# Inverse roots by one GpSimd power, front loads on two hardware DMA queues, and a written-out order per engine, in a fused attention and GELU-MLP kernel

## The chip, the core and the metric

The kernel runs on one core of a Trainium2 chip. The metric is device time in microseconds (us) from launch to end; the median of three runs is compared. The engines of the core are named as the profile names them: PE (TensorE matmuls; PEld its weight loads), DVE (VectorE), ACT (ScalarE), POOL (GpSimd) and SP (SyncE, which here only issues DMAs). Each engine works through its own list of instructions in order and waits for others by semaphores.

## The reference

What is computed, cut to its core (batch 8, 12 heads, sequence 448, head size 64; then 3584 tokens of 768, inner size 2048):

```python
def rmsnorm(x, g):
    rms = np.sqrt(np.mean(x * x, axis=-1, keepdims=True) + 1e-06)
    return x / rms * g
q_n, k_n = rmsnorm(q, g_q), rmsnorm(k, g_k)
scores = np.matmul(q_n, k_n.transpose(0, 1, 3, 2)) / np.sqrt(64)
attn = softmax(scores)
x = np.matmul(attn, v)            # heads side by side: (3584, 768)
h = x @ w_in                      # (768, 2048)
g = h * (1.0 / (1.0 + np.exp(-1.702 * h)))
out = g @ w_out                   # (2048, 768)
```

## The kernel before

Two heads of one batch form a pair; there are 48 pairs, six to a batch. The kernel is written as a list of small tasks. Each task names its engine, the tasks it depends on, a duration that a planner assumes, and the code that issues its instructions. `_Order.run` plays these tasks through with the assumed durations, always takes the ready task of lowest key on each engine, and issues instructions in that order. So the finished program is a static list on each engine; keys (`KEYS`), earliest times (`AT`) and a set of moved tasks (`ON`) steer it. Where the planner finds PE idle, `fill` (L1047) puts dummy matmuls of zeros.

Names of tasks for pair i (used in the texts below):

- L(i,0), L(i,1), L(i,2): load q, k, v from memory, 224 KB each (L1065, L1062), on SP's DMA queue; L(0,1) alone and the two tiny loads of g_q and g_k go out on ACT's queue.
- S: squares (ACT L1073, or POOL L1070 in two halves). R: sum over a row of 64 (DVE L1082). Q: inverse root. For pairs 0 to 5, one at a time, it is Ln and Exp on ACT (L1093, L1094); for later pairs, three at a time, a seed by integer arithmetic on DVE (L1101, L1103) and two Newton steps of four instructions on POOL (L1114 to L1117).
- N(i,0), N(i,1): q and k times the inverse root, to bfloat16 (L1124, on POOL or DVE). V: v to bfloat16 (L1134 DVE, L1137 POOL).
- T(i,0), T(i,1): transposes, on PE (L1147) for pairs 0 to 11, by DMA (L1159) later. KQ, K: copies of the transposed q and k out of PSUM, k times the gains (L1151, L1154).
- C: scores (PE L1194), E: their exponential (ACT L1204 for pairs 0 to 5, which are done in two halves h = 0, 1 of the queries; L1202 later), P: times v (PE L1215), O: division by the row sum (DVE L1225, L1226), B and X: transpose back and copy into the tokens' matrix xt (PE L1241 and DVE L1245, later by DMA L1248).
- WI(c), WO(c): four loads each of w_in and w_out with conversion to bfloat16, issued by POOL (L1396, L1402).
- F(b,m): first product for batch b, block m (PE L1429), H: tanh (ACT L1439), G: gate (DVE L1451). Then the second product (PE L1459, L1524), written in large part as Strassen-like products of sums, which DVE forms; copies out on ACT and DVE, stores on SP and ACT (L1482).

F(b,m) needs all six pairs of batch b. So at the start PE has only the attention of the first six pairs; from F(0,0) on, attention of later pairs stands between the products of earlier batches.

ACT's function table is loaded at the start (set 6, for Ln and Exp), again after the Q of pairs 0 to 5 (set 0, for Exp and tanh), and near the end (set 12, for the last GELU).

The functions around the change:

Of the kernel before, what the change touches and what calls it, by code (L numbers as in the profile page):

```python
# [19 lines left out]
class _Task:  # L20
    __slots__ = ("eng", "dur", "lat", "emit", "key", "after", "at", "takes", "left", "users", "end", "start", "lock", "widen", "moves", "rest", "there", "alt", "either")


OVERLAP = {"ACT": 95.0, "DVE": 90.0, "POOL": 45.0}


class _Order:

# [12 lines left out]
    def add(self, name, eng, dur, emit, key, deps=(), lat=100.0, at=0.0, takes=None,  # L41
            lock=False, widen=None, moves=None, alt=None, either=None):


        t = _Task()
        t.alt = alt

        lat += OVERLAP.get(eng, 0.0)
        if name in ON:
            eng, dur, lock = alt  # L50
        dur -= OVERLAP.get(eng, 0.0)
        if alt:
            t.alt = alt[0], alt[1] - OVERLAP[alt[0]], alt[2]
        t.eng, t.dur, t.lat, t.emit = eng, dur, lat, emit
        t.after, t.at, t.takes = tuple(deps), AT.get(name, at), takes
        t.users, t.end, t.lock, t.widen = [], None, lock, widen
        t.moves = moves
        t.either = either and (either[0], either[1] - OVERLAP[either[0]],
                               lat - OVERLAP.get(eng, 0.0) + OVERLAP[either[0]], either[2])
        t.key = KEYS.get(name, round(key, 3))  # L60
        self.tasks.append(t)
        self.named[name] = t

    def run(self):
        for t in self.tasks:
            t.left = 0
            for d in t.after:
                if d in self.named:
                    self.named[d].users.append(t)
                    t.left += 1  # L70
        ready = {}
        seq = 0
        events = []
        free = {}

        def push(t, when):
            nonlocal seq
            seq += 1
            heapq.heappush(events, (when, seq, t))

        for t in self.tasks:
            ready.setdefault(t.eng, [])
            free.setdefault(t.eng, 0.0)
            if t.left == 0:
                push(t, t.at)
        free.setdefault("POOL", 0.0)
        self.free, self.hold = free, 0.0
        now, emitted = 0.0, 0
        over = []

        queues = {"sw": [], "hw": [], "act": []}
        moved_to = 0.0

# [3 lines left out]
        def share(t):  # L97
            n = len(heads())
            if n != 2:
                return 1.0 / n  # L100
            return 0.65 if not queues["sw"] else 0.69 if t.eng == "POOL" else 0.47

        def next_moved():
            h = heads()
            when = [q[0].there for q in queues.values() if q and q[0].there > moved_to]
            when += [moved_to + t.rest / share(t) for t in h]
            return min(when) if when else None

        def move_to(now):
            nonlocal moved_to, seq  # L110
            while moved_to < now:
                n = next_moved()
                until = now if n is None else min(now, n)
                h = heads()
                for t in h:
                    t.rest -= (until - moved_to) * share(t)
                moved_to = until
                for q in queues.values():
                    while q and q[0].rest < 1e-3 and q[0].there <= moved_to:
                        t = q.pop(0)  # L120
                        t.end = moved_to + 500.0
                        seq += 1
                        heapq.heappush(over, (t.end, seq, t, False))

        while emitted < len(self.tasks):
            for eng, q in ready.items():
                while q and free[eng] <= now:
                    held = []
                    best = None
                    while q:  # L130
                        c = heapq.heappop(q)
                        if c[2].end is not None:
                            continue
                        if self._fits(c[2], now):
                            best = c[2]
                            break
                        held.append(c)
                    for c in held:
                        heapq.heappush(q, c)
                    if best is None:  # L140
                        break
                    if best.either and eng != best.eng:
                        best.eng, best.dur, best.lat, best.emit = best.either
                    best.either = None
                    if best.takes and best.takes[0] in self.loose:
                        held = self.slots[best.takes[0]][1]
                        self.got = min(self._open(best.takes[0], now),
                                       key=lambda j: held[j] and self.named[held[j]].end or 0.0)
                        held[self.got] = best.takes[1][0]
                    elif best.takes:  # L150
                        self.slots[best.takes[0]][1].extend(best.takes[1])
                    for name, n in best.widen or ():
                        self.slots[name][0] = n
                    if eng == "PE" and self.fill:
                        self.fill(now - free[eng], now)
                    best.emit()
                    emitted += 1
                    free[eng] = now + best.dur
                    if best.lock:
                        self.hold = free[eng]  # L160
                    best.start = now
                    seq += 1
                    heapq.heappush(over, (free[eng], seq, best, True))
                    if best.moves:
                        best.rest, best.there, best.end = best.moves, free[eng] + 1850.0, 1e12
                        queues[{"POOL": "sw", "ACTQ": "act"}.get(eng, "hw")].append(best)
                    else:
                        best.end = free[eng] + best.lat
                        seq += 1
                        heapq.heappush(over, (best.end, seq, best, False))  # L170
            nxt = []
            if events:
                nxt.append(events[0][0])
            if over:
                nxt.append(over[0][0])
            nxt += [f for f in list(free.values()) + [self.hold] if f > now]
            n = next_moved()
            if n is not None:
                nxt.append(n)
            assert nxt, "no task can start"  # L180
            now = max(now, min(nxt))
            move_to(now)
            while over and over[0][0] <= now:
                _, _, t, same = heapq.heappop(over)
                for u in t.users:
                    if (u.eng == t.eng and not u.either) == same:
                        u.left -= 1
                        if u.left == 0:
                            push(u, max(now, u.at))
            while events and events[0][0] <= now:  # L190
                _, _, t = heapq.heappop(events)
                seq += 1
                for eng in (t.eng, t.either[0]) if t.either else (t.eng,):
                    heapq.heappush(ready[eng], (t.key, seq, t))
        move_to(now + 1e6)
        return now

    def _open(self, name, now):
# [3 lines left out]
        back = [h and self.named[h].end for h in held]  # L202
        return [j for j, h in enumerate(held)
                if h is None or (back[j] is not None and back[j] <= now)]

    def _fits(self, t, now):

        if (t.lock and self.free["POOL"] > now) or (t.eng == "POOL" and self.hold > now):
            return False
        if not t.takes:  # L210
            return True
        if t.takes[0] in self.loose:
            return bool(self._open(t.takes[0], now))
        n, held = self.slots[t.takes[0]]
        for j in range(len(t.takes[1])):
            if len(held) + j >= n:
                back = self.named[held[j - n]]
                if back.end is None or back.end > now:
                    return False
        return True  # L220

KEYS = {
    'Lg': 22.65, 'g': -13.05, 'gT': -31.93, 'gG': -13.06, ('L', 0, 0): -4.25, ('L', 0, 1):
# [633 lines left out]
def kernel(  # L859
# [166 lines left out]
    def fill(idle, now):  # L1026
        if waiting:
            idle -= waiting.pop()
# [975 lines left out]
```

## Time and profile before

| | us |
|---|---|
| timed runs: median (lowest to highest of 3) | 418.61 (417.22 to 418.70) |
| profiled execution: span from first to last instruction | 417.8 |
| PE busy in it | 406.2 |
| DVE, ACT, POOL busy | 316.9, 297.8, 177.4 |
| 113 dummy matmuls of L1047, busy | 18.3 |

The profiled execution is one run apart from the timed ones; the profile gives its span, and no separate time around it. "Busy" of PE includes the dummy matmuls and the pipelined ends of matmuls. Data moved: 45.61 MB read from memory and 11.01 MB written.

### The profile page before, as it was taken

The numbers are of one execution on the slowest core, as the hardware profiler recorded it, in microseconds if no ns is written. First come the engines' busy times: TensorE is split into PE (matmuls) and PEld (weight loads), VectorE is DVE, ScalarE is ACT, GpSimd is POOL, SyncE is SP. The second block draws the span as 40 slices with busy tenths as digits, with TensorE's granted clock in tenths as the row PEclk, the third lists the DMA queues.
The fourth block names the chain that finished last, engine by engine and source line by source line (L and its number), as shares of the span: only waits on it lengthen the run. The fifth ranks groups of instructions, "written<-read, shape, count | busy, mean of one in ns | idle before, by whom it ended". The sixth has DMA issues, their size and how long they took to land.

```text
span 417.8 us, 10076 instructions
## 1 busy us (share of the span) xinstructions
PE 406.2 (97%) x3874; PEld 240.4 (58%) x3874; DVE 316.9 (76%) x640; ACT 297.8 (71%) x441; POOL 177.4 (42%) x271
## 2 busy tenths in 40 slices
PE   8799999999999999999999999999999999999996
PEld 6557876655555555565555555455555665555564
DVE  3968888859979879887898877788757699557432
ACT  4879778789978588966997658886887725773211
POOL 5784978491565047937447164664220000000000
PEclk9999999999999999999999999999999999999999
DMA  8999999966385789588874787855541231000323
GB/s 202 232 245 245 257 242 249 245 183 158 79 192 126 174 210 225 108 230 183 191 190 121 164 207 201 160 110 139 136 111 35 54 99 57 2 1 16 99 77 113
DMA packets 101716, 63.38 MB, mean 152 GB/s; under 512 B 54948, under 2 KB 101668, under 8 KB 101668
## 3 DMA queue, kind: packets, MB, share of 16 engines
q1 hardware_dynamic: 93520, 55.58, 56.0%
q0 software_dynamic: 7296, 6.29, 9.2%
q10 hardware_dynamic: 852, 0.87, 0.7%
q8 instruction: 30, 0.49, 0.5%
q14 instruction: 18, 0.15, 0.1%
HBM read 45.61 MB, written 11.01 MB: 136 GB/s over the span
## 4 chain that ended last, share of the span: by engine, by line
PE 75%; DVE 8%; DMA 4%; ACT 4%; POOL 4%; issue 4%; SPq 0%; DVEq 0%; POOLq 0%; ACTq 0%
PE w L1429 20%; PE w L1524 19%; PE o L1215 10%; PE sc L1194 9%; PE b L1524 5%; PE b L1813 4%; PE w L1813 4%; PE w L1459 3%; DMA rows<-in_k_dram 3%; DMA rows<-in_v_dram 2%; DVE ssq L1082 2%; ACT att L1204 1%; ACT att L1202 1%; POOL row L1124 1%; POOL sq L1070 1%
## 5 line engine op out<-in xcount | busy, mean ns | idle before, releaser
L1202 ACT ACTIVATE att<-sc 112x896 bf16<-112x896 f32 x168 | 145.4, 916 | 28.1 <-PE sc L1194 27.2
L1429 PE MATMUL w<-xt,w_in_s 128*128 128x448 bf16 (+1 forms) x672 | 119.8, 326 | 1.0 <-DVE xt L1245 0.9
L1429 PEld LDWEIGHTS <-w_in_s 128*128 128x128 bf16 x672 | 61.2, 98 | 43.0 <-issue 8.3
L1215 PEld LDWEIGHTS <-att 112*128 112x128 bf16 x1536 | 61.6, 98 | 28.0 <-issue 9.7
L1451 DVE SCALAR_TENSOR_TENSOR g<-th,w 128x448 bf16<-128x448 f32 x96 | 57.9, 615 | 23.0 <-ACT th L1439 22.6
L1124 POOL TENSOR_TENSOR row<-rows,rs 112x512 bf16<-112x512 f32 x64 | 67.5, 1074 | 17.5 <-DMA qk<-row 14.1
L1082 DVE TENSOR_REDUCE ssq<-sq 112x16 f32<-112x1024 f32 (+1 forms) x50 | 58.0, 1169 | 9.6 <-ACT sq L1073 8.4
L1439 ACT ACTIVATE th<-w 128x448 f32<-128x448 f32 x96 | 51.6, 548 | 18.7 <-PE w L1429 16.7
L1215 PE MATMUL o<-vx,att 112*128 112x65 bf16 x1280 | 58.9, 194 | 0.9 <-ACT att L1204 0.6
L1194 PE MATMUL sc<-qk 64*128 64x448 bf16 (+1 forms) x360 | 47.0, 342 | 1.3 <-ACT att L1202 0.7
L1070 POOL TENSOR_TENSOR sq<-rows 112x512 f32<-112x512 f32 x29 | 29.7, 1042 | 36.6 <-DMA rows<-in_q_dram 15.3
L1137 POOL TENSOR_TENSOR vx<-rows,ones 112x512 bf16<-112x512 f32 x20 | 21.5, 1075 | 54.3 <-PE o L1215 45.6
L1226 DVE TENSOR_TENSOR obs<-o,rcp 112x256 bf16<-112x256 f32 x96 | 40.7, 424 | 3.5 <-DVE rcp L1225 0.2
L1524 PEld LDWEIGHTS <-late 128*128 128x128 bf16 x304 | 27.9, 98 | 21.3 <-issue 3.6
L1524 PEld LDWEIGHTS <-g 128*128 128x128 bf16 x288 | 26.4, 98 | 19.1 <-issue 3.2
L1073 ACT ACTIVATE sq<-rows 112x1024 f32<-112x1024 f32 (+1 forms) x31 | 31.3, 1017 | 7.3 <-DMA rows<-in_q_dram 4.4
L1225 DVE RECIPROCAL rcp<-o 112x4 f32<-112x4 f32 x96 | 16.9, 176 | 15.9 <-PE o L1215 15.2
L1524 PE MATMUL w<-w_out_s,late 128*128 128x384 bf16 x152 | 28.5, 327 | 0.1
L1524 PE MATMUL w<-w_out_s,g 128*128 128x384 bf16 x152 | 28.3, 326 | 0.0
L1524 PE MATMUL w<-late 128*128 128x384 bf16 x128 | 24.1, 326 | 0.1
L1204 ACT ACTIVATE att<-sc 112x896 bf16<-112x896 f32 x24 | 20.8, 918 | 3.9 <-PE sc L1194 3.9
L1114 POOL TENSOR_TENSOR t<-rs 112x48 f32<-112x48 f32 x28 | 9.6, 344 | 31.6 <-DVE rs L1103 30.1
(132 smaller groups left out, 517.3 us busy)
## 6 DMA issues: line engine op xcount, KB each, us to landing
rows<-in_q_dram SPq DMA_DIRECT2D x44, 224.0 KB, 3.8
rows<-in_k_dram SPq DMA_DIRECT2D x43, 224.0 KB, 4.2
rows<-in_v_dram SPq DMA_DIRECT2D x42, 224.0 KB, 3.4
w_in_s<-in_moe_w_in_dram POOLq DMA_DIRECT2D x4, 768.0 KB, 15.2
w_out_s<-in_moe_w_out_dram POOLq DMA_DIRECT2D x4, 768.0 KB, 20.5
out_dram<-osb SPq DMA_DIRECT2D x10, 168.0 KB, 3.0
out_dram<-osb SPq DMA_DIRECT2D x14, 120.0 KB, 2.1
out_dram<-osb SPq DMA_DIRECT2D x11, 144.0 KB, 2.2
```

What stands on the lines that cost most here:

```text
L1070: nc.gpsimd.tensor_tensor(out=sq[i % N_SQ][:SS, g], in0=raw[turn(i, N_RAW, K_RAW)][:SS, g], in1=raw[turn(i, N_RAW, K_RAW)][:SS, g], op=ALU ...
L1082: nc.vector.reduce_sum(out=ssq_of[g0][:SS, i - g0, part], in_=sq[i % N_SQ][:SS, part], axis=AX.X)
L1124: eng.tensor_tensor(out=row_ring[i % N_QKN][:SS, gi].rearrange("p n (h d) -> p h n d", h=2), in0=raw[turn(i, N_RAW, K_RAW)][:SS, gi], in1= ...
L1194: nc.tensor.matmul(sc[:, hp, j * SH:j * SH + n], lhsT=qkw[r, k0:k0 + WIN], rhs=qk[r, 0, qs], start=True, stop=True)
L1202: nc.scalar.activation(out=att[:SS, t, :, :S], in_=sc, func=ACT.Exp)
L1215: nc.tensor.matmul(os_[u, w][:, x, :], lhsT=att_of(u)[:SS, kc, hp, qs * SS:qs * SS + WIN], rhs=vx_ring[turn(i, N_V, K_V)][:SS, hp, kc, :], ...
L1226: nc.vector.tensor_tensor(out=to[:SS, :, w, :] if h is None else to[:SS, :2].rearrange("p n h d -> p (n h) d"), in0=o[:SS, :, :D], in1=rcp ...
L1429: nc.tensor.matmul(gps[b, m][:, j * SH:j * SH + n], lhsT=w_in_s[:, ki, f * 128:(f + 1) * 128], rhs=xT[b][:, ki, lo:lo + n], start=(ki == 0 ...
L1439: nc.scalar.activation(out=th[:, :], in_=gps[b, m][:, :S], func=ACT.Tanh, scale=0.851)
L1451: nc.vector.scalar_tensor_tensor(out=g_of[b // 2][:, f:f + len(g), lo:lo + n], in0=view(ths.pop((b, m))[:, :]), scalar=1.0, in1=view(gps.p ...
L1524: nc.tensor.matmul(held[to], lhsT=lhs[:, ko, :], rhs=y[:, ko, :], start=first and ko == 0, stop=ko == NK - 1, skip_group_check=not first)
L1813: nc.tensor.matmul(joint[n, to][:, :S], lhsT=w[:, ki, n * 128:(n + 1) * 128], rhs=x[:, ki, :], start=first and ki == 0, stop=ki == KH - 1, ...
```

## The change

1. Q is one instruction on POOL: the sum to the power -0.5 (`ALU.pow` with a tile of -0.5). The square tiles `sq` get a 65th column that holds 64e-6, so the sum R contains the epsilon. Ln, Exp, seed and Newton steps are gone, and so is one of ACT's table loads: set 0 is loaded at the start.
2. Any of the loads L of pairs 0 to 11 may go out on ACT's DMA queue; 13 do. The two tiny loads of g_q and g_k go out on POOL's.
3. The order on each engine is a written-out list (`ORDER`); `run` now only walks these lists with assumed durations, to decide buffers and dummy matmuls (86 instead of 113) and the order of issue between engines. Which engine a task runs on follows from the list that holds it (`PLACE`). The earliest times of WI and WO are gone. Some assumed durations differ.

The diff, cut to its core:

```diff
-    table(6)
+    table(0)
+    for j, src in enumerate((g_q, g_k)):
+        nc.gpsimd.dma_start(out=gqk[:, j], in_=src.rearrange("(o d) -> o d", o=1))
...
-    sq = ring("sq", N_SQ, [128, 2, 2, NS, D], FP32)
+    sq = ring("sq", N_SQ, [128, 2, 2, NS, D + 1], FP32)
+    for t in sq:
+        nc.vector.memset(t[:, :, :, :, D:D + 1], float(D) * 1e-6)
+    power = consts.tile([128, 3, 2, 2, NS], FP32)
+    nc.vector.memset(power[:, :, :, :, :], -0.5)
...
+        eng = nc.scalar if ("L", i, which) in ON else nc.sync
...
-        nc.scalar.activation(out=x, in_=x, func=ACT.Ln, bias=eps[:SS, :])
-        nc.scalar.activation(out=y[:SS], in_=x, func=ACT.Exp, scale=-0.5)
...
-        for _ in range(2):
-            eng.tensor_tensor(out=t, in0=yg, in1=yg, op=ALU.mult)
-            eng.tensor_tensor(out=t, in0=t, in1=x, op=ALU.mult)
-            eng.tensor_scalar(out=t, in0=t, scalar1=1.5, scalar2=None, op0=ALU.add)
-            eng.tensor_tensor(out=yg, in0=yg, in1=t, op=ALU.mult)
+        nc.gpsimd.tensor_tensor(out=y[:SS, :n], in0=x, in1=power[:SS, :n], op=ALU.pow)
...
-    od.add("Lg", "ACTQ", 820, load_g, -4.0, at=1300.0, lat=4000.0)
-    od.add("g", "DVE", 270, scale_g, -1.95, deps=["Lg"], lock=True)
+    od.add("g", "DVE", 270, scale_g, -1.95, at=6000.0, lock=True)
...
-        od.add(("WI", c), "POOL", 1050, lambda c=c: load_in(c), -50, at=12000.0 + 4500.0 * c,
-               deps=[("WI", c - 1)], moves=4400.0)
+        od.add(("WI", c), "POOL", 1050, lambda c=c: load_in(c), -50, deps=[("WI", c - 1)], moves=4400.0)
...
-            if b == m == 0:
-                od.add("table", "ACT", 1500, lambda: table(0), 3.0,
-                       deps=[("Q", p) for p in range(NP)])
```

The heads of the new lists, as far as the opening goes:

```python
ORDER = {
  'SP': [L(0,1), L(1,1), L(3,1), L(2,0), L(4,1), L(1,2), L(4,0), L(5,0), L(5,1), L(6,0), L(6,1),
         L(3,2), L(8,0), L(4,2), L(5,2), L(10,2), L(7,0), L(7,1), ...],
  'ACT': [L(0,0), L(1,0), L(3,0), L(2,1), L(0,2), S(0,0), S(0,1), S(1,0), S(1,1), S(2,0), S(3,0),
          E(0,0,0), S(4,0), E(0,0,1), L(2,2), S(5,0), E(1,0,1), E(1,0,0), E(2,0,1), E(2,0,0),
          E(3,0,0), E(3,0,1), E(4,0,0), E(4,0,1), L(10,0), E(0,1,0), E(0,1,1), E(5,0,1), E(5,0,0),
          E(1,1,0), E(3,1,0), E(1,1,1), E(2,1,0), E(3,1,1), E(2,1,1), L(11,1), L(9,0), L(6,2),
          S(8,0), E(4,1,0), H(0,1), ...],
  'POOL': [Q(0), N(0,1), WI(0), Q(1), N(1,0), Q(2), N(2,0), N(2,1), Q(3), N(3,1), Q(4), N(4,0),
           WI(1), N(4,1), Q(5), N(5,0), N(5,1), S(6,0), WI(2), S(7,0), WI(3), Q(8), N(6,0), ...],
  'DVE': [R(0,0), R(0,1), 'g', R(1,1), N(0,0), 'gG', R(1,0), KQ(0), R(2,0), K(0), V(1), R(3,0),
          N(1,1), KQ(2), KQ(1), V(0), R(4,0), K(1), N(3,0), O(0,0,0), K(2), R(5,0), KQ(3), K(3),
          V(2), X(0,0), O(1,0,0), KQ(4), K(4), O(2,0,0), V(3), V(4), X(1,0), KQ(5), O(3,0,0), K(5), ...],
  'PE': ['gT', T(0,0), T(0,1), C(0,0,0), T(1,0), T(2,0), T(1,1), C(0,0,1), P(0,0,0,*), T(2,1),
         C(1,0,1), C(1,0,0), C(2,0,1), T(3,0), T(3,1), C(2,0,0), B(0,0), ...,
         C(1,1,1), C(2,1,0), B(0,1), B(5,0), C(3,1,1), P(1,1,0,*), C(2,1,1), F(0,0), C(4,1,0), ...],
}
```

(Names are shortened here: L(0,1) is written `('L', 0, 1)` in the code, and the star stands for four tasks.)

## The prediction

> **What bounds the kernel now.** I read the page's first table first.
>
> ```profile
> span 417.8 us, 10076 instructions
> PE 406.2 (97%) x3874; PEld 240.4 (58%) x3874; DVE 316.9 (76%) x640; ACT 297.8 (71%) x441; POOL 177.4 (42%) x271
> ```
>
> TensorE (PE) looks full, but 113 of its matmuls are dummies of `fill` (L1047), put where it would be idle. So I asked for PE's busy time by stretch (columns: stretch, length, busy and count, clock, DMA share, GB/s):
>
> ```profile
> 0.00:20.00 20.00, 16.45 (x161) 1.00 1.01 216
> 20.00:40.00 20.00, 18.58 (x257) 1.00 1.18 245
> ...
> 60.00:410.00 350.00, 348.17 (x3171) 1.00 0.59 138
> ```
>
> and for the dummies alone (a column for weight loads comes in):
>
> ```profile
> 0.00:20.00 20.00, 11.98 (x72) 8.06 (x72) 1.00 1.01 216
> 20.00:40.00 20.00, 5.88 (x38) 2.99 (x38) 1.00 1.18 245
> ```
>
> In the first 40 us real matmuls take (16.45 - 11.98) + (18.58 - 5.88) = 17.2 us, so 22.8 us are lost; from 60 to 410 us only 1.8 us. No matmul of the result is added or dropped. Time can come only from the opening, from single stalls, or from the 4 us after PE's end. PE's timeline dates the opening and the largest stall:
>
> ```profile
> 9.54 0.57 PE L1147 MATMUL w<-ident,row 112*128 112x112 bf16 x8
> ...
> 36.10 1.31 PE L1429 MATMUL w<-xt,w_in_s 128*128 128x224 bf16 x12
> ...
> 54.06 1.98 PE L1429 MATMUL w<-xt,w_in_s 128*128 128x224 bf16 x19 [0.90 <-DVE xt L1245]
> ```
>
> The first transpose stands at 9.54, the first projection F(0,0) at 36.10; from there PE is mostly full. The chain of waits names who leads in between (start, length, what):
>
> ```profile
> 2.67 6.31 DMA rows<-in_k_dram
> 9.00 7.82 DMA rows<-in_v_dram
> ...
> 27.44 1.28 ACT L907
> ...
> 43.30 2.04 POOL row L1124 x2
> ```
>
> Loads, then ScalarE (ACT; the 1.28 is a change of its function table), then GpSimd (POOL). Why loads lead, the DMA view of 0 to 12 us shows; its slices are 0.3 us:
>
> ```profile
> GB/s 0 0 0 0 0 14 164 116 212 338 379 380 345 213 242 212 232 242 222 253 253 205 266 222 219 263 215 239 242 222 253 215 239 249 208 259 236 219 253 222
> ...
> q1 hardware_dynamic: 2344, 2.25, 86.1%
> q10 hardware_dynamic: 244, 0.23, 5.8%
> ```
>
> q1 is SyncE's (SP's) queue, q10 ACT's. While ACT's one load ran, 338 to 380 GB/s moved; on SP's queue alone it is about 235. A load of 229 KB then takes 0.98 us.
>
> **What the Trainium skill says.** "DMA: Bandwidth & Descriptors", section "Issuing engines are not separate DMA queues": starting DMAs from several engines saves only the issue time. The slices above disagree by a factor of 1.5; I follow them. "ScalarE: Activation LUTs", section "What ACT_TABLE_LOAD costs": about 1,283 ns and a drain of about 1,380. The trace has the 1.28, and the next activation starts at 28.74, so no drain is seen. "GPSIMD Engine Reference", section 3.1: about 2.6 cycles per element of a two-input operation at 1.2 GHz, 1.11 us for 512; the trace has 1,074 ns (L1124). No page prices a power.
>
> **The change part by part.**
>
> *Inverse roots.* Six pairs of Ln and Exp (0.31 + 0.21 us on ACT, 3.1 us in all) and the table load of 1.28 go: 4.4 us of ACT before F(0,0). For 14 groups of three pairs, eight Newton rows on POOL (344, 300, 328 and 286 ns, twice; 40.31 to 43.30 with gaps, 2.99 us) and two seed rows on DVE (0.19 each) go. In come 20 powers on POOL, 6 of 16 elements and 14 of 48. Nothing shows a power. From below: the plain 48-element row, 0.3 us. From above: the eight rows it replaces, 2.7 us. I take 0.8 for 16 elements and 1.5 for 48, a guess between these ends. The epsilon column makes a reduction 65 long instead of 64, 1.6% of 1.2 us on DVE, beside other work.
>
> *Opening.* I walk the new order with the trace's durations. Loads L(0,0) on ACT and L(0,1) on SP replace the same pair of queues, so they land at 5.1 and 4.8 as now. ACT then issues two more loads (each waits for a lane, one of eight in rotation, and takes 0.4) before its first square: 5.5 instead of 4.79. Two squares (0.6 each, overlapping by little) and DVE's reductions (0.69) end at 7.4 (now 6.73); power 0.8; normalizing, one half on DVE (0.69), one on POOL (1.04), ends at 9.3 against 9.48. But R(2,0) (1.21) now stands ahead of K(0) on DVE, also `g` (0.78) and R(1,1) ahead of N(0,0): K(0) ends near 12.5, and the first score comes 1.6 us later than now (10.95).
>
> Behind it the new order gains. ACT's queue carries 6 of the first 18 loads, 1.37 MB at its 158 GB/s beside SP's 195 (packets of 3 to 4 us), so what lands at 18.9 lands at 2.7 + 8.7 + 4.5 = 15.9. ACT is what is late next: four squares to 7.9, S(2,0) and S(3,0) when loads 2 and 3 are there (9 to 11), then E(0,0,0) at 13, and from E(1,0,1) at 18.8 one exponential of 0.9 after another with a square or load issue between. DVE keeps ahead of it: K(1) at 18.25, K(2) 20.0, K(3) 22.1, K(4) 24.5, K(5) 28.1, the last just before E(5,0,1). E(2,1,0), behind which F(0,0) stands on PE, ends at 33.9; F(0,0) starts at 34.3. At 36.10 the kernel before has the same 17 exponentials behind it. Gain 1.8 us, by its ACT count (20 begun at 35.7, now 19 at 37.4) 2.6. I take **2.2**, ends -1 and 4.
>
> *Weights.* W_in's transfers (WI) start at 9.4 instead of 12.0, but the fourth issue moves from 24.7 to some 30.8, behind squares on POOL. The first issue took 5.9 us to move bytes, a transfer 6.8. The fourth lands near 46.4 (now 45.1), and F(0,6), its first user, is due at 45.7. Cost **0.5**, ends 0 and 3. The two small loads of g_q and g_k go from ACT to POOL, beside its memsets, before POOL has any other work: nothing.
>
> *The stall at 51.5 to 54.* PE loses 1.7 us there (starts of matmuls further apart than usual), 1.07 of it before the 54.06 row. It is the end of the POOL chain: Newton to 43.30, then rows, casts and squares without a break. Now Q(8) comes after S(8,0) on ACT (35.7), its reduction at 38, and ends at 39.5, 3.7 us earlier. I take **1.5** of the 1.7. What could be late next is DVE's share of rows; it falls by 8.
>
> *Fixed order.* Both programs are static; the order is another one on every engine. Beside the above, four stalls of 0.3 to 1.1 us (69, 95, 228, 253 us; 2.7 in all) belong to the old order, and a new order may have its own. I take a gain of **0.7**, ends 2.7 and -4. Work on DVE (14 x 0.38, some 0.69 rows) and POOL that goes after 60 us is hidden by PE, whose busy 348.17 of 350 is the cover; if PE stalled there it would count. Stores, dummies (27 fewer, in idle time) and tail: nothing, within 0.5.
>
> Sum: 2.2 - 0.5 + 1.5 + 0.7 = 3.9 us, from 418.6 to **414.7**. The profiled execution shows its span of 417.8 alone; the median of the timed runs, 418.61, is 0.8 above it, which I let stand as what lies around it.
>
> **Rivals.**
>
> *The power is dear* (ends slower). POOL is full from 7.4 to 24.6 in my walk: six powers 4.8, nine rows 9.4, two WI issues 2.0, together 16.2 of 17.2. All of PE's opening passes through it. K(5) has 2.6 us of room. Each power dearer by x delays E(5,0,1) by 6x - 2.6; the gain of 3.9 is gone at x = 1.1, a power of 1.9 us. At the upper end of 2.7 the loss is 9.1 us, and the time 419.9, more if later powers hold rows of the next batch: 420 to 424. For it: nothing shows the price. Against: its eight predecessors are one vector operation each. Chance 0.14.
>
> *New stalls* (slower). The order interleaves ACT's loads and exponentials; a load issue that waits for its lane holds all exponentials behind it. With transfers near 1.9 us each while W_in flows (SP's 120 of 245 GB/s), a few such waits of 1 to 2 us, or K(1) late, cancel the opening's gain and more: 421 to 423. For: ACT issues 13 loads instead of one. Against: lanes are eight deep, and I find the earlier load on each early lane landed. Chance 0.10.
>
> *The front moves but nothing follows* (no change). Loads come sooner, yet W_in lands no earlier, so F(0,6) waits and the opening's 2.2 is given back, with one new stall: 417 to 419. Chance 0.15. That the two queues bring nothing is the same case: the later first score then stands alone.
>
> *Forecast:* 411 to 416.5. Chance 0.61.
>
> **How the numbers follow.** A difference of 0.5%, about 2.1 us, is what a measurement here can tell. The forecast's cases lie below 416.5: faster 0.61. The third rival is within: 0.15. The first two: slower 0.24. The range reaches from 410 (opening 4, all old stalls gone, less 0.3) to 421.5, which takes in no change and about half of the slower cases.
>
> **What would show it.** Right: one load each on two queues at 340 to 380 GB/s over the first 10 us; 20 powers of about 0.8 and 1.5 us; F(0,0) near 34.3 although the first score is at about 12.5; ACT without gaps from 19 us; no stall at 51 to 54; PE full from 60 us. Wrong: a power over 1.9 us; F(0,0) after 36; a row of PE waiting for w_in_s; PE losing over 4 us after 60 us.

## The result, and the profile after

The changed kernel takes **501.97 us** (median of 4 runs, 500.16 to 503.15), the kernel before 418.0 beside it: a ratio of 1.2015, interval 1.1978 to 1.2053. I had forecast 414.7, with 410.0 to 421.5 as the range. It is slower by 84 us.

I read the page of the changed kernel in the order in which the prediction reads the old one. First the busy times, then three rows of the 40 slices (tenths busy; PEclk is the clock granted to PE):

```profile
span 501.4 us, 9854 instructions
...
PE 430.7 (86%) x3847; PEld 251.6 (50%) x3847; DVE 322.3 (64%) x608; ACT 289.3 (58%) x424; POOL 295.4 (59%) x196
...
PE   7569497867797969987979699987799999999995
...
POOL 6994758695839296999195894497959200000000
PEclk8777889786898989997999899999899999999999
```

PE, mostly full from 36 us before, now has holes as long as POOL has work (the first 32 slices), and none after. POOL has 75 instructions fewer and 118 us more busy time. What fills it, the groups of instructions by shape on POOL show (busy us, mean ns of one, idle before):

```profile
L877 POOL TENSOR_TENSOR rs<-ssq,power 112x48 f32<-112x48 f32 x14 | 113.0, 8072 | 53.3 <-DVE ssq L865 52.9 <-DMA qk<-row 0.3
...
L877 POOL TENSOR_TENSOR rs<-ssq,power 112x16 f32<-112x16 f32 x6 | 17.9, 2987 | 3.3 <-DVE ssq L865 3.3
```

One power of 48 elements takes 8.07 us, one of 16 takes 2.99. The prediction had 1.5 and 0.8. From the two, (8,072 - 2,987) / 32 = 159 ns an element. PE's busy time by stretch (length, busy and count, clock, DMA share, GB/s) stands against the same three rows of before:

```profile
0.00:20.00 20.00, 11.85 (x81) 0.89 1.01 234
20.00:40.00 20.00, 14.32 (x164) 0.67 0.58 119
60.00:410.00 350.00, 303.08 (x2805) 0.92 0.60 136
```

From 60 to 410 us PE is busy 303 of 350 us where it was 348. The loss is not in the opening alone, and the clock has fallen too, so even "busy" time is worth less. The Trainium skill, "TensorE: Matmul & The Clock Gate", Part 1, has the clock halved after an idle window. This trace fits that: the clock is 1.00 from 12.4 to 19.2 us, in which PE works 2.79 of 6.8 us, then 0.50 to 26.0, and 1.00 again to 32.8; 0.67 is the mean of 20 to 40 us, where the kernel before had 1.00. The view of waits says who is late (us in total, times, longest):

```profile
POOL rs L877 <- DVE ssq L865: 56.2, 12, 10.8
...
DVE row L884 <- POOL rs L877: 35.2, 9, 6.3
...
PE w L907 <- POOL row L884: 21.9, 8, 6.7
```

The first row is the surprise: POOL, the engine with the dear operation, itself waits 56 us for sums of squares. The chain of work that ended last shows why that is no slack:

```profile
PE 38%; POOL 34%; issue 15%; DVE 6%; DMA 4%; SPq 1%; ACT 0%; POOLq 0%; DVEq 0%; ACTq 0%
```

```profile
52.46 8.04 POOL rs L877
...
70.85 2.30 DVE ssq L865 x2
76.82 8.04 POOL rs L877
85.82 5.05 POOL row L884 x5
91.47 2.24 PE w L1177 x12
100.55 8.05 POOL rs L877
109.87 6.26 DVE row L884
```

(Start, length, what; only the longest pieces are listed.) Square, sum, power, rows, attention, products, and again: the stages of one group of three pairs follow one another, and the engines wait for each other in turn. Two links close the ring. In the same chain, between the first two powers shown, the sums on DVE (70.85 us) stand behind copies of transposed rows (69.57), and POOL comes to its next power only behind these sums. And SP waits 66.3 us for POOL's rows before it issues loads of q and k (12.1 in the kernel before). In that ring a longer power is paid in time, however low the engine's share.

The opening, from PE's timeline (start, length, idle before):

```profile
8.80 0.22 PE L1021 MATMUL w<-ones,g_row 1*128 1x1 f32 x1 [1.97 <-DVE g_row L1013]
...
11.53 0.71 PE L907 MATMUL w<-ident,row 112*128 112x112 bf16 x5
...
14.49 0.36 PE L954 MATMUL sc<-qk 64*128 64x224 bf16 x4 [0.76 <-DVE qk L914]
...
48.12 1.32 PE L1177 MATMUL w<-xt,w_in_s 128*128 128x224 bf16 x12
```

First transposes at 11.53 (9.54 before), first score at 14.49 (10.95), F(0,0) at 48.12 (36.10; forecast 34.3). Even the tiny product with g waits, for a reason of its own: see the sixth experiment.

### The profile page after: what moved, and what is told of

It is laid out like the page before. It is cut to its first block, busy times and chain, and to the rows that moved or that the text cites. A ratio compares the mean times of both kernels' runs of the same rounds, so it can differ in the third digit from the quotient of the medians.

```text
span 501.4 us, 9854 instructions
## 1 busy us (share of the span) xinstructions
PE 430.7 (86%) x3847; PEld 251.6 (50%) x3847; DVE 322.3 (64%) x608; ACT 289.3 (58%) x424; POOL 295.4 (59%) x196
## 4 chain that ended last, share of the span: by engine, by line
PE 38%; POOL 34%; issue 15%; DVE 6%; DMA 4%; SPq 1%; ACT 0%; POOLq 0%; DVEq 0%; ACTq 0%
POOL rs L877 19%; PE w L1272 11%; POOL row L884 8%; PE w L1177 8%; PE b L1272 5%; POOL sq L853 5%; PE o L975 5%; PE b L1561 4%; PE sc L954 3%; PE w L1561 2%; DMA rows<-in_q_dram 2%; DVE row L884 2%; DVE ssq L865 2%; DMA qk<-row 1%; POOL vx L897 1%
## 5 line engine op out<-in xcount | busy, mean ns | idle before, releaser
L877 POOL TENSOR_TENSOR rs<-ssq,power 112x48 f32<-112x48 f32 (+1 forms) x20 | 130.9, 6547 | 56.6 <-DVE ssq L865 56.2
L1177 PE MATMUL w<-xt,w_in_s 128*128 128x448 bf16 (+1 forms) x672 | 128.6, 339 | 17.5 <-DVE g L1199 17.5
L975 PEld LDWEIGHTS <-att 112*128 112x128 bf16 x1536 | 71.2, 103 | 49.8 <-issue 19.0
L884 POOL TENSOR_TENSOR row<-rows,rs 112x512 bf16<-112x512 f32 x71 | 79.2, 1134 | 7.7 <-DMA qk<-row 6.6
L865 DVE TENSOR_REDUCE ssq<-sq 112x16 f32<-112x1040 f32 (+1 forms) x50 | 59.0, 1185 | 17.1 <-POOL sq L853 11.3
L975 PE MATMUL o<-vx,att 112*128 112x65 bf16 x1280 | 66.8, 199 | 3.0 <-POOL vx L897 2.9
L1199 DVE SCALAR_TENSOR_TENSOR g<-th,w 128x448 bf16<-128x448 f32 x96 | 57.1, 615 | 16.4 <-ACT th L1187 15.9
L853 POOL TENSOR_TENSOR sq<-rows 112x512 f32<-112x512 f32 x40 | 43.8, 1115 | 15.7 <-DVE ssq L865 11.6
L954 PE MATMUL sc<-qk 64*128 64x448 bf16 (+1 forms) x360 | 50.0, 359 | 1.4 <-DVE qk L914 0.8
L884 DVE TENSOR_TENSOR row<-rows,rs 112x512 bf16<-112x512 f32 x17 | 17.6, 1044 | 23.2 <-POOL rs L877 23.2
L856 ACT ACTIVATE sq<-rows 112x1024 f32<-112x1024 f32 (+1 forms) x26 | 25.6, 994 | 10.8 <-DVE ssq L865 3.8
```

The lines of the kernel that those rows point to most:

```text
L853: nc.gpsimd.tensor_tensor(out=sq[i % N_SQ][:SS, g, :, :, :D], in0=raw[turn(i, N_RAW, K_RAW)][:SS, g], in1=raw[turn(i, N_RAW, K_RAW)][:SS, ...
L865: nc.vector.reduce_sum(out=ssq_of[g0][:SS, i - g0, part], in_=sq[i % N_SQ][:SS, part], axis=AX.X)
L877: nc.gpsimd.tensor_tensor(out=y[:SS, :n], in0=x, in1=power[:SS, :n], op=ALU.pow)
L884: eng.tensor_tensor(out=row_ring[i % N_QKN][:SS, gi].rearrange("p n (h d) -> p h n d", h=2), in0=raw[turn(i, N_RAW, K_RAW)][:SS, gi], in1= ...
L954: nc.tensor.matmul(sc[:, hp, j * SH:j * SH + n], lhsT=qkw[r, k0:k0 + WIN], rhs=qk[r, 0, qs], start=True, stop=True)
L975: nc.tensor.matmul(os_[u, w][:, x, :], lhsT=att_of(u)[:SS, kc, hp, qs * SS:qs * SS + WIN], rhs=vx_ring[turn(i, N_V, K_V)][:SS, hp, kc, :], ...
```

## The experiments

Times are medians; the kernel before had 417.5 to 418.2 beside the groups. Where the power is replaced by a multiplication, the inverse root is left out and only the shape of the work is kept.

**1. The power made cheap.**

```diff
-    nc.vector.memset(power[:, :, :, :, :], -0.5)
+    nc.vector.memset(power[:, :, :, :, :], 1.0 / 512)
...
-  nc.gpsimd.tensor_tensor(..., in1=power[:SS, :n], op=ALU.pow)
+  nc.gpsimd.tensor_tensor(..., in1=power[:SS, :n], op=ALU.mult)
```

> The changed kernel with one edit: the POOL instruction of the inverse root multiplies by 1/512 instead of taking the power -0.5 (same operands and shapes, same place in every engine's list). It leaves the inverse root out: the factor is the row's sum over 512, which is 0.125 for an average row. Theory 1, the loss is the price of the power (2.99 us for 16 elements, 8.07 for 48, 130.9 us in all): the row falls to about 0.3 us and the time to 412 to 418, near the forecast of 414.7, with PE full from 60 us on. Theory 2, the new order or the loads on two queues are what is slow: the time stays over 440.

Measured: **428.74** (ratio 1.0232, 1.0174 to 1.0290). So the twenty powers cost 73.2 of the 84 us. The other 11 us were forecast as a gain of 3.9. With an operation cheaper than I had assumed, the order and the queues still lose: two errors, not one. F(0,0) is at 39.03.

**2. One queue.** On the kernel of experiment 1:

```diff
-        eng = nc.scalar if ("L", i, which) in ON else nc.sync
+        eng = nc.sync
```

> The kernel with the product in place of the power (inverse root left out, as before), and besides all loads of q, k and v issued on SP's queue in the same order of issue. It tells what the second queue is worth. Theory 1: the opening loses what the two queues gave, 1.5 to 4 us over the product kernel, and 213 to 263 GB/s in the first 12 us instead of 250 to 300. Rival, the transfers bound later work only through W_in, or ACT's issue time costs as much as the second queue gives: within 1 us of the product kernel or faster.

Measured: **426.31** (1.0189, 1.0130 to 1.0249). The second queue brings nothing; without it the median is 2.4 us better, though the ranges overlap a little (427.29 to 428.84, and 425.86 to 428.00). The DMA view of 0 to 12 us gives the same amount moved, experiment 1 first:

```profile
DMA packets 2637, 2.47 MB, mean 206 GB/s; under 512 B 229, under 2 KB 2637, under 8 KB 2637
```

```profile
DMA packets 2670, 2.50 MB, mean 208 GB/s; under 512 B 230, under 2 KB 2670, under 8 KB 2670
```

Its slices say where my reading went wrong. First this kernel, all loads on one queue, 0 to 12 us in slices of 0.3; then the changed kernel, 10 to 20 us in slices of 0.25:

```profile
GB/s 0 0 0 0 0 17 184 256 314 273 348 209 195 164 116 147 143 263 324 280 229 256 215 270 266 229 246 294 239 242 290 229 259 277 242 246 290 236 242 300
```

```profile
GB/s 262 287 279 274 266 275 274 254 291 279 242 287 262 270 258 283 262 254 279 274 258 275 279 262 258 234 201 213 213 217 205 197 205 209 213 221 201 197 213 217
```

Slices over 310 GB/s come on one queue too, at the start of the transfers. And from 11.5 to 15 us, when the loads on ACT's queue have landed, SP's alone moves 242 to 291. Two queues share what one can carry, so each transfer on them takes longer: in experiment 1 the loads of pair 0 land at 4.7 and 5.0 us, with one queue at 3.7 and 4.5, and the twelfth load lands at 14.6 and 14.8. L(2,1), fourth on ACT's queue, lands at 11.7 in experiment 1, and ACT waits 3.84 us for it with S(2,0). The Trainium skill, "DMA: Bandwidth & Descriptors", section "Issuing engines are not separate DMA queues", has DMAs of all engines run on the same 16 DMA engines; these traces agree with it.

**3. The power alone, in the kernel before.** Ln and Exp stay for the first six pairs; the 14 later groups get it in place of Newton.

```diff
-  nc.vector.tensor_scalar(out=x, ..., scalar1=float(D) * 1e-6, scalar2=-0.5, op0=ALU.add, op1=ALU.mult)
-  nc.vector.tensor_scalar(out=y..., scalar1=-0.5, scalar2=..._MAGIC..., ...)
+  nc.vector.tensor_scalar(out=x, ..., scalar1=float(D) * 1e-6, scalar2=None, op0=ALU.add)
...
-  for _ in range(2):  # four instructions each
+  eng.tensor_tensor(out=yg, in0=x, in1=power[:SS, :len(grp)], op=ALU.pow)
```

> The kernel before with one part of the change: the 14 inverse roots of three pairs are one POOL power of 48 elements in place of eight Newton instructions, with the epsilon added by one DVE instruction in place of the two of the seed; the first six pairs keep Ln and Exp, the order and the queues stay. Theory 1: each batch of three pairs is about 5 us later on POOL (8.07 against 2.99), POOL's busy time goes from 177 to about 255, and the time rises by 10 to 45 us, mostly as stalls of PE after 40 us. Theory 2 (the order is at fault, POOL has room for the power): within 3 us of 418.

Measured: **475.48** (1.1361, 1.1285 to 1.1436): 57.8 us more, above all that was expected. Its group row on POOL:

```profile
L1111 POOL TENSOR_TENSOR rs<-ssq,power 112x48 f32<-112x48 f32 x14 | 112.8, 8056 | 29.8 <-DVE ssq L1103 29.3 <-DVE rcp L1219 0.2
```

A group is 8.06 - 2.99 = 5.07 us longer than Newton with its gaps, 71 us in all, and 81% of that reaches the end. POOL was 42% busy in this kernel. PE's 97% was no cover.

**4. The planner told the measured price.**

```diff
-            od.add(("Q", i), "POOL", 800 if i < NP else 1500, ...
+            od.add(("Q", i), "POOL", 2980 if i < NP else 8070, ...
```

> The changed kernel with one edit: the planner is told 2980 and 8070 ns for the power instead of 800 and 1500. The lists per engine stay; only the choice of buffers, the dummy matmuls and the interleaving of issue follow. Theory 1, the time is the power's own on a fixed chain: within 2% of 502, dummies in the gaps raise the granted clock from 0.92 towards 1 and take at most 10 us off. Rival, a good part of the loss is the lower clock and buffers chosen for times that do not come: under 485.

Measured: **497.41** (1.1883, 1.1816 to 1.1951). The order of the tasks is fixed, so only buffer choices and dummy matmuls change; the mean clock goes from 0.92 to 0.96. 4.6 of 84 us: a wrong price in the planner is not the cause.

**5. Only the first six powers.** The changed kernel, with the multiplication for the groups of three (`if n == 1:` keeps the power).

> The changed kernel with the power kept for the first six pairs (16 elements each) and a multiplication by 1/512 in place of the 14 powers of 48 elements: the inverse root of pairs 6 to 47 is left out. It splits the 73 us that the twenty powers cost (502.0 against 428.7 with twenty multiplications). Theory 'the opening pays for six in a row': six powers of 2.99 us, about 18 us on GpSimd between the first transposes and the first projection, delay that projection from 39.0 to about 48 us, and the loss stays to the end: 428.7 + 9 = 438, ends 435 and 443; the 14 later powers then cost the other 64 us. Rival 'the opening hides it' (the later stages are so far behind that what the opening loses is not the bound): below 432.

Measured: **435.64** (1.0431, 1.0403 to 1.0459). The six powers cost 435.64 - 428.74 = 6.9 us; F(0,0) moves from 39.03 to 47.96. The 14 later ones cost the other 501.97 - 435.64 = 66.3 us, 4.7 us each of the 7.8 by which they are longer than the multiplication.

**6. The g loads back on ACT.** On the kernel of experiment 2: `nc.gpsimd.dma_start(out=gqk...` becomes `nc.scalar.dma_start`.

> The kernel of the second experiment (multiplication in place of the power, the inverse root left out; all loads on SyncE's queue) with the two small loads of g_q and g_k issued by ScalarE again, as in the kernel before, and not by GpSimd. Theory 'the small loads by GpSimd land late and hold VectorE': VectorE's row of g no longer waits (1.65 us of idle with the multiplication), the rows of pair 0 come earlier, and the first projection moves from 38.1 to 36.5 to 37.5 us: 424.3 to 425.8. Rival 'a nothing, as the prediction had it': 425.9 to 426.7, the first projection at 38 still.

Measured: **426.14** (1.0202, 1.0175 to 1.0229), F(0,0) at 38.49: the rival held. The local fact is real: the two loads of 0.2 KB took 6.0 and 6.2 us to landing in the changed kernel, DVE's row of g (at 8.47) waited 1.21 us for them, and with ACT issuing it stands at 6.42 without a wait. Another wait is behind it, and the time stays.

**7. Two rows from DVE to POOL.** On that kernel, N(13,0) and N(12,1) leave DVE's list and stand behind N(12,0) on POOL's. The reason is this stretch of the changed kernel, DVE first (idle before in brackets), then POOL beside it:

```profile
108.63 0.69 DVE L884 TENSOR_TENSOR row<-late,rs 112x512 bf16<-112x512 f32 x1 [6.32 <-POOL rs L877]
...
109.79 6.35 DVE L884 TENSOR_TENSOR row<-late,rs 112x512 bf16<-112x512 f32 x1
```

```profile
109.55 1.05 POOL L884 TENSOR_TENSOR row<-late,rs 112x512 bf16<-112x512 f32 x1
...
114.55 1.03 POOL L897 TENSOR_TENSOR late<-late,ones 112x512 bf16<-112x512 f32 x1
```

The same DVE instruction takes 0.69 us and, started inside a run of six POOL operations without a gap, 6.35; it ends 0.56 us behind the last of them. In experiments 1 and 2 it took 6.19 and 6.18 at 78 and 76 us and ended 0.55 us behind, so it is not the power.

> The kernel of the experiment with g on ScalarE, and the two rows that VectorE normalizes at about 76 and 83 us (pair 13 first half, pair 12 second half) put on GpSimd, behind pair 12's first half; the inverse root is left out as there. With them on VectorE one of the two lasts 6.2 us where 0.69 is usual, beside six GpSimd operations in a row. Theory 'the two engines get in each other's way': no VectorE instruction is long there, the 3.3 us stall of TensorE at about 82 us goes, and the time falls by 2 to 4 us. Rival 'that VectorE row was waiting for something else': another VectorE instruction is long at the same place and the time stays within 1 us.

Measured: **422.61** (1.0131, 1.0091 to 1.0171), 3.5 us better. No DVE instruction is long there any more, although POOL's run is two operations longer, and PE is busy 39.72 of 40 us between 60 and 100 (36.09 before the edit).

**8. Newton on DVE in the kernel before, first six pairs.** In place of Ln and Exp, two seed and six Newton operations of 16 elements.

> The kernel before, whole, with one edit: the inverse roots of the first six pairs by two seed operations and six Newton operations on VectorE (16 elements each) at the place in the program where ScalarE's Ln and Exp stood; the planner's costs are left as they are. It takes the 4.4 us of Ln, Exp and table load off ScalarE and adds some 1.2 us a pair to VectorE. Theory 'ScalarE's opening work is worth what the prediction took it for': the first projection moves from 36.1 to 34 to 35.5 us and the time falls by 0.5 to 2 us (415.7 to 417.2). Rival 'the old order does not use it' (ScalarE waits for loads and rows in that stretch, and VectorE's 7 us more come in between): no gain, 417.5 to 420.

Measured: **425.97** (1.0202, 1.0179 to 1.0226), 8.5 us worse, far outside both expectations. DVE has eight operations of 0.17 us, 1.6 us a pair, 10 us over six pairs; F(0,0) moves from 36.10 to 44.50. The edit took less off ACT than I expected: Ln and Exp are gone (3.1 us), but the table load stayed in, at 35.43 us. ACT now waits up to 3.4 us at a time for scores between 13 and 33 us, so what it was freed of found no use; what DVE was given came out at the end almost whole. The two are changed together here; experiment 12 gives ACT's part apart from DVE's.

**9. K(0) ahead of R(2,0) on DVE.** On the kernel of experiment 7, one exchange in the list.

> The kernel of the experiment with the two rows on GpSimd (multiplication in place of the power, so the inverse root is left out), with one pair of VectorE's list exchanged: the first pair's K(0) ahead of R(2,0). The prediction saw R(2,0) stand ahead of K(0) and priced it at 1.6 us of the first score; the traces have R(2,0) waiting for the load of pair 2, and the first score at 14.6 where the kernel before has 10.95. Theory 'that one queue position holds the opening': the first score comes at about 11.7, ScalarE's first exponential 2.9 us earlier, the first projection 1 to 2.5 us earlier (37 to 38), and the time falls from 422.6 to 420 to 421.7. Rival 'the later loads and squares lead, not the first score': the first score moves, the first projection stays at 39, the time stays within 0.7 us of 422.6.

Measured: **422.43** (1.0090, 1.0057 to 1.0123; runs 420.79 to 424.0), against 422.61 no clear difference (the intervals overlap). The first score does move, from 14.98 to 11.81, and F(0,0) from 39.24 to 37.10. PE then loses 1.09 us at 40 and 1.25 us at 70 us, the second waiting for W_out. The theory was right on the position; its worth for the whole time does not show.

**10. The old roots in the new order.** On that kernel: Ln and Exp for pairs 0 to 5, seed and Newton for the groups, as in the kernel before. The whole computation is done.

> The kernel of the experiment with K(0) ahead of R(2,0), with the inverse roots of the kernel before put into its order at the power's place: Ln and Exp on ScalarE for the first six pairs, two seed operations on VectorE and eight Newton operations on GpSimd for each group of three. The whole computation is done. Theory 'the power alone made the changed kernel slow, the order and the older roots go together': the six pairs of Ln and Exp with their table load cost 2 to 4 us in the opening, Newton on GpSimd (2.7 us more a group than one multiplication) nothing after 60 us: 422.5 to 425.5. Rival 'the order has no room for Newton either' (GpSimd's 14 x 2.7 us delay rows in places): 428 to 435. In no case below the kernel before at 417.5.

Measured: **444.89** (1.0635, 1.0598 to 1.0672), a miss of both, for a reason that neither theory has: the new kernel loads function table 0 at its start, where the old one loads table 6, which holds Ln and Exp together. Twelve table loads of 1.28 us came in, 15.4 us of ACT before 37 us; F(0,0) is at 48.49.

**11. More dummies.** On the kernel of experiment 9, FILL 1.2 to 1.8 and FILL_GAPS 0.6 to 1.2.

> The kernel of the experiment with K(0) ahead of R(2,0) (the inverse root left out) with more dummy matmuls in TensorE's idle time of the opening: FILL 1.2 to 1.8, FILL_GAPS 0.6 to 1.2. In the traces of this order the clock is 0.58 from 16 to 20 us and 0.70 from 28 to 32 us, behind stretches with little work. Theory 'the granted clock costs time in the opening': the clock stays at 1.00 in each stretch, the first projection comes 0.5 to 1.5 us earlier and the time falls by 0.5 to 1.5 us. Rival 'dummies stand ahead of work': the clock rises, the first projection comes no earlier, the time stays or grows by up to 1.5 us.

Measured: **423.07** (1.0112, 1.0073 to 1.0150). The clock is 1.00 in the first 20 us (0.91 without), but 0.91 from 20 to 40 (1.00 without), so the theory's condition was met in the first half only. F(0,0) comes at 39.36, later than 37.10. A full clock in the first 20 us is not what the opening lacks; for the rest this run doesn't decide.

**12. Experiment 10 with the right table.** Table 6 at the start, table 0 behind the sixth Exp.

> The kernel of the experiment with the older inverse roots in the new order, whole, with the function table held as the kernel before holds it: one table with both Ln and Exp loaded at the start, and one change of table behind the sixth pair's Exp. Without this each of the 12 Ln and Exp of the run before brought a table load of 1.28 us (15.4 us of ScalarE between 8.9 and 36.7 us; first projection at 48.5). Theory 'the table loads were what it lost': ScalarE's opening has 4.4 us of root work as the kernel before has, the first projection is at 39 to 42.5, and the time 423 to 430. Rival 'Newton and its seeds do not fit the new order': GpSimd's Newton waits on VectorE's seeds (TensorE lost 3.0 us at 55.8 behind it) in many places, and the time is 432 to 440.

Measured: **436.42** (1.0446, 1.0421 to 1.0471); the rival held. F(0,0) is at 37.51, against 37.10 without any root: Ln, Exp and the table change, put back, cost the opening 0.4 us. But PE then stops. Its timeline, and POOL's beside it:

```profile
50.01 0.56 PE L926 MATMUL w<-ident,row 112*128 112x112 bf16 x4 [2.83 <-POOL row L903]
```

```profile
45.42 0.26 POOL L893 TENSOR_TENSOR t<-rs 112x48 f32<-112x48 f32 x1 [3.78 <-DVE rs L888]
...
48.04 0.28 POOL L896 TENSOR_TENSOR rs<-rs,t 112x48 f32<-112x48 f32 x1
48.40 1.55 POOL L903 TENSOR_TENSOR row<-late,rs 112x512 bf16<-112x512 f32 x1
```

The group's last sum ends on DVE at 43.96, the seed, behind two gates on DVE, at 45.33. Newton's eight instructions lie from 45.42 to 48.3, and the row behind them is what PE waits for. Against experiment 9 the two kinds of root cost 14.0 us. Against the kernel before, which has the same roots, this order is 18 us slower (436.42 and 418.17): it has no room even for the 4.4 us that lie here between the sum and the rows.

**13. Two rows ahead of a value copy.** On the kernel of experiment 9, near 277 us: POOL is idle for 3.3 us ahead of V(38), then runs V(38), N(43,0), N(44,1). The edit puts the two rows first. DVE's timeline without the edit, then with it:

```profile
277.44 1.51 DVE L1269 TENSOR_TENSOR late<-g 128x1024 bf16<-128x1024 bf16 x1
278.87 1.11 DVE L934 TENSOR_SCALAR qk<-qk,gG 128x448 bf16<-128x448 bf16 x1
...
280.50 1.53 DVE L1269 TENSOR_TENSOR late<-g 128x1024 bf16<-128x1024 bf16 x1
```

```profile
276.14 0.69 DVE L1271 TENSOR_TENSOR late<-g 128x1024 bf16<-128x1024 bf16 x1
276.75 1.12 DVE L936 TENSOR_SCALAR qk<-qk,gG 128x448 bf16<-128x448 bf16 x1
...
278.39 0.68 DVE L1271 TENSOR_TENSOR late<-g 128x1024 bf16<-128x1024 bf16 x1
```

> The kernel of the experiment with K(0) ahead of R(2,0) (the inverse root left out), with one exchange in GpSimd's list near 277 us: the two rows of pairs 43 and 44 ahead of the value copy of pair 38, which waits for TensorE. GpSimd is idle for 3.3 us ahead of that copy and then runs three operations in a row, beside which four VectorE operations take 1.1 to 1.5 us where 0.33 to 0.69 is usual, and TensorE loses 2.5 us (0.6, 0.5 and 1.5). Theory 'contention again': with the rows in the idle time, VectorE's operations there have their usual lengths, the stall of 2.5 us shrinks to under 1 us and the time falls by 1 to 2.5 us. Rival 'TensorE waits there for another reason': VectorE's operations get short and the stall stays over 1.5 us; the time within 0.8 us of 422.4.

Measured: **420.13** (1.0048, 1.0023 to 1.0072), 2.3 us better. PE's loss there, by the starts of its matmuls, falls from 2.5 to 0.9 us. One operation (1.12) still falls beside a POOL row. DVE's operations got short and the stall went with them, so its cause is shown. Its size is less sure than the 2.3 us: the profiled executions also differ at 41 and 71 us, where the edit changes nothing (idle times of 0.92 and 1.08 us on PE without it, 0.21 and none with it).

Put together, each step being the difference of two medians (the kernel before, beside them, moved by 0.7):

| from 501.97 | us |
|---|---|
| 14 powers of 48 elements | -66.3 |
| 6 powers of 16 elements | -6.9 |
| second queue | -2.4 |
| g loads by POOL | -0.2 |
| DVE rows beside POOL's run, 78 us | -3.5 |
| K(0) behind R(2,0) | -0.2 |
| DVE beside POOL, 277 us | -2.3 |
| left over against the kernel before (418.17) | -2.0 |

The two steps of 0.2 can't be told from nothing. No version beats the kernel before: the best one leaves the inverse root out and still is 0.5% slower. The last row is therefore not all that the order loses. With the same roots as the kernel before (experiment 12, with the edits of experiments 2, 6, 7 and 9 in it) it loses 18 us.

## Why the prediction was wrong, step by step

*The power's price.* Wrong, and the main error. The step that failed is the bound from above: "the eight rows it replaces, 2.7 us". What eight plain operations take says nothing of a ninth kind; that was the upper end of my hopes, not of the operation. Measured: 2.99 and 8.07 us. (The bound was not read rightly either: the eight rows add to 2.5 us, 2.99 with their gaps.) I took one range for both sizes, too; my 0.8 and 1.5 make 22 ns an element where the two measured sizes make 159.

*POOL after 60 us "is hidden by PE".* Wrong. I named PE's 348.17 of 350 as cover and priced 14 of 20 powers at nothing. Experiments 3 and 5 show 4.1 us of each 5.1 and 4.7 of each 7.8 reaching the end. A full PE shows that nothing is late today, not how much later the others may be. A better guide would have been the time between a group's sum and the first use of its rows; no run here tests that guide.

*The rival "the power is dear"* named the mechanism and had 0.14. Its place was right and its size nearly so in the opening: 6x - 2.6 with x = 2.99 - 0.8 gives a delay of 10.5 us; measured are 8.9 at F(0,0) and 6.9 in the time. Its sum at the upper end is wrong: with x = 2.7 - 0.8 the formula gives 8.8 us, not 9.1, and the time 414.7 + 8.8 = 423.5, not 419.9. It stopped at 424, because later powers were left out of the number there as well.

*Two queues at 340 to 380 GB/s.* Wrong. Four slices of 0.3 us at the start of the transfers were read as a rate. Between 5 and 8 us, kernels with two queues moved 242 to 280 GB/s (the changed one and experiments 1, 4 and 5), kernels with one 236 to 279 (the one before and experiments 2, 3, 6 and 9). The loads that I wanted at 15.9 instead of 18.9 do come early in the changed kernel (the tenth at 11.5 and the sixteenth at 16.6, with 12.9 and 18.9 before), but kernels on one queue differ as much from each other: in experiment 3 the tenth lands at 11.7. In experiment 1, with W_in issued earlier, the sixteenth lands at 21.7. So the gain of 2.2 in the opening had no ground. I had the page that said so and set a burst against it.

*First score 1.6 us later.* Right in its cause, R(2,0) ahead of K(0), and short in size: 3.5 us in the changed kernel. There the first transposes are already 2.0 us late, and R(2,0) stands between KQ(0) and K(0) with its 1.2. Without the power it is R(2,0) that leads: it waits for the load of pair 2, where I had let it run when DVE was free, and the exchange of the two takes 3.2 us away (experiment 9, 14.98 to 11.81). That it hardly matters (experiment 9) is the third rival, the front moves and nothing follows, in small.

*ACT's 4.4 us out of the opening.* They went, and bought next to nothing: put back in experiment 12 they cost F(0,0) 0.4 us. With the cheap operation F(0,0) is at 39.03, and ACT waits for scores (gaps of 0.8, 0.5 and 1.6 us between 20 and 28 us in experiment 9), where I saw it without gaps from 19.

*g loads on POOL: nothing.* The step was wrong in itself (landing 6 us after issue, DVE waits), right in its effect on the time.

*Weights, 0.5.* No wait for W_in stands among PE's waits in the changed kernel. But the earlier issue has a cost that I did not price. In experiment 1 W_in is issued at 8.9 us instead of 12.0, and from the fourteenth load on q, k and v land 1.8 to 2.3 us apart instead of 1.0; the sixteenth comes at 21.7 us, later than the 18.9 of before. I saw that W_in slows loads to 1.9 us each and used it only in a rival. Whether this is what holds F(0,0) at 37 to 39 us, behind 36.10, was not tested: no run puts the earliest times back.

*The stall at 51.5 to 54.* With the real power Q(8) runs from 52.46 to 60.50 and the step is void. Without the power it runs at 42.88 (experiment 9; I had 39.5), and PE is busy 19.99 of 20 us from 40 to 60 in experiment 7 (19.07 in experiment 9), 18.92 in the kernel before. With the root left out, up to 1.1 of the 1.5 were there to be had.

*Fixed order: gain 0.7, ends 2.7 and -4.* Wrong in sign. The order brought two stalls of 3.5 and 2.3 us, both of a kind that I had not looked for: DVE and POOL beside each other. The diff even shows the planner's answer to it, `lock`, which in the model keeps a DVE row off POOL's work; a list that is fixed per engine keeps it only as long as the model's times come true. What stays behind these two is open: 2 us with the root left out, and with the old roots, for which the order was not laid out, 18 us in all, of which one stall is traced (experiment 12, 50 us).

## What to carry to other kernels

Before an operation takes the place of several, get its price at the size used, or let the range reach far above the old cost; "one instruction for eight" says nothing of time. Don't price a longer step by its engine's share or by another engine's being full, and look for the slack between its input and its first user instead: here, on an engine that was 42% busy, four fifths of each added microsecond were paid. And read a DMA rate from several microseconds in which more than one transfer is running, never from the first burst.

## What the runs showed of the hardware

- A power on GpSimd: 2.99 us for 16 elements a partition, 8.07 for 48, beside 0.22 and 0.28 in most cases for a multiplication of the same shapes (experiment 1).
- A DVE operation with two inputs from SBUF, 0.69 us alone, takes 5.1 to 6.35 us when it starts inside six POOL operations without a gap, and ends 0.55 us behind the last of them (the changed kernel and experiments 1, 2 and 6); beside one or two it takes up to 1.5. The one that starts first keeps its length: at 10.31 us in the changed kernel DVE's row takes 0.69 us, and POOL's, begun 0.04 us later, 1.55 instead of 1.04. The Trainium skill, "GPSIMD Engine Reference", section 1, names the shared SBUF interfaces and contention with such DVE instructions; the size is from these runs. A bfloat16 operation with one tensor and a column of scalars (L934, 0.33 to 1.11) is slowed as well.
- A load of 0.2 KB issued by GpSimd at the start took 6.0 to 6.9 us to landing in kernels with two queues, 4.3 and 4.7 with one.
- One hardware queue carried 242 to 291 GB/s with loads of 224 KB (changed kernel, 11.5 to 15 us); over 5 to 8 us five kernels with one queue moved 236 to 279, four with two queues 242 to 280.
